# A three-stage transformer kernel on one core: the prologue and the first token tile rebuilt, with the second product of that tile in float32

## The chip, the cores and the metric

The kernel runs on one NeuronCore of a Trainium2 chip. The metric is the device time of one execution in microseconds. Five engines work side by side, each through its own instructions in order: TensorE (PE in the profile; PEld is its weight load), VectorE (DVE), ScalarE (ACT), GpSimd (POOL) and SyncE (SP), which here issues all the transfers between device memory and the chip. An instruction that has to wait holds up everything behind it on its engine.

## The reference

All inputs are float32. B = 8, S = 576 tokens, 8 heads of 64, model width 512, inner width 1024. Cut to what is computed:

```python
q_c = q.reshape(B, H, 9, 64, D)                  # k, v likewise: attention inside chunks of 64 tokens
scores = scale * q_c @ k_c.T; scores -= max(scores)
attn = exp(scores); attn /= sum(attn) + 1e-9
x = (attn @ v_c), heads side by side             # [B, S, 512]

h = max(x @ w_in, 0)                             # stage two, 512 -> 1024
conv_out = sum over k of conv_w[k] * h shifted by k - 1 tokens
x = (h * sigmoid(conv_out)) @ w_out              # 1024 -> 512

h = max(x @ w_in2, 0); u, v = halves of h        # stage three
x = (u * (w_spatial @ layernorm(v) + b_spatial)) @ w_out2
```

## The kernel before

**Products.** A float32 product is made of three products in the rounded type float32r: a matrix is kept as a rounded high part and a low part (the full value less the high part), and a product is high·high + low·high + high·low. The high part is a ScalarE copy (`nc.scalar.copy`, L127, L428, L353), the low part a subtraction (`split_lo`, L68) on VectorE or GpSimd.

**Weights.** They arrive as 64-bit words and are converted on the chip, in pieces of 128 x 512 (`Pieces`, L102): a load into `raw` (L111), a ScalarE scaling into `nr` (L78), two VectorE steps, a shift (L82) and a shift-and-or (L86), together called a merge here, and then the high and the low part. `w1` is the matrix of x @ w_in, `w2` that of the product behind the gate; eight pieces each. `w3` and `w4` belong to stage three.

**Phase A** does attention and stage two, `phase_b` stage three. Phase A walks through 11 token tiles of 384 or 448 tokens; a tile takes 8 slots, one for each 128 columns of the inner width. In slot s, `moe_in` does 12 matmuls into `h` (L381), `moe_h` (L387) makes on ScalarE max(h, 0) (L393) and the middle tap (L395), and on VectorE the outer two taps (L408); one slot later `moe_g` does tanh on ScalarE (L419) and the gate's product on VectorE (L420); a slot later `moe_split` makes the parts `gh`, `gl`; and in slot s + 3 (`LAG`) `moe_out` adds 12 matmuls into four accumulators `acc` (L441).

**Attention** goes by groups of 128 tokens, three or four groups a tile, and runs ahead of the tiles: `att_s` (scores on TensorE, L197), `sm1_steps` (row maximum, L210, then for the first six groups only a scaled negative maximum, L214, and for later ones a subtraction, L217), `att_exp` (for the first six groups eight ScalarE instructions with that bias, L233; one instruction for later ones, L237), `sm2_steps` (sum L247, a small constant L250, reciprocal L253, scaling L256), a transposition (`att_tp` on TensorE, L292, with a ScalarE copy, L296, for the first six groups; VectorE and eight transfers, L265 and L274, for later ones) and `att_pv` (L333 or L346), whose result `xh`, `xl` feeds `moe_in`.

**Order.** The order on every engine is the order of the code. A prologue (from L471) issues the loads, dummy matmuls on zeros (`keep_warm`, L467), the attention of groups 0 to 2 and the first pieces of w1. `start_slot` (L552) writes slots 0 to 8, in which the weights of stage two are still being converted: in slot s piece s + 1 of w1 and piece s - 1 of w2, roughly. In these slots the low parts of w1, w2 and g are subtractions on GpSimd, and the third tap of the convolution is a ScalarE product (L403) and a GpSimd addition (L413). The tables `S_SLOT` and `PV_SLOT` (L46) say in which slot the scores and the last product of groups 3 to 8 stand. Later slots are written by the loop at L579.

Of the kernel before, what the change touches and what calls it, by code (L numbers as in the profile page):

```python
# [7 lines left out]
F32 = mybir.dt.float32  # L8
# [10 lines left out]
DM = 512  # L19
# [21 lines left out]
LAG = 3  # L41
AHEAD = 3
VBUFS = 4
NP = 6
RBUFS = 5
S_SLOT = {3: 0, 4: 1, 5: 2, 6: 6, 7: 8, 8: 10}  # L46
# [14 lines left out]
def attention_moe_kernel(ctx: ExitStack, tc: tile.TileContext, qT, kT, vL, vP, eye, w1, cw, w2, w3, wsp, wsr, bsp, w4, out):  # L61
# [40 lines left out]
    class Pieces:  # L102
        def __init__(self, pool, items, bufs=2, nbufs=2):
            self.pool, self.items, self.bufs, self.nbufs = pool, items, bufs, nbufs
            self.raw, self.scaled, self.merged = [], [], []

        def load(self, n=1):
            for _ in range(min(n, len(self.items))):
                src, a, m, h, l = self.items.pop(0)
                raw = self.pool.tile([128, a, m], U64, tag="raw", name="raw", bufs=self.bufs)  # L110
                nc.sync.dma_start(out=raw, in_=src)  # L111
                self.raw.append((raw, a, m, h, l))

        def scale(self, n=1):
            for _ in range(min(n, len(self.raw))):
                raw, a, m, h, l = self.raw.pop(0)
                self.scaled.append((scale_word(self.pool, raw, a, m, self.nbufs), h, l))

        def merge(self, n=1):
            ps, self.scaled = self.scaled[:n], self.scaled[n:]  # L120
            self.merged += [(w[0], h, l) for w, h, l in ps]
            return merge_steps(*[w for w, _, _ in ps])

        def split(self, eng=nc.gpsimd):
            while self.merged:
# [18 lines left out]
    def phase_a(mid):  # L144
# [6 lines left out]
        es_st = ExitStack()  # L151
        st = es_st.enter_context(tc.tile_pool(name="start", bufs=1, side="right"))
# [7 lines left out]
        w2l = wp.tile([128, KF, DM], F32R, name="w2l")  # L160

# [25 lines left out]
        def att_s(g):  # L187
# [4 lines left out]
            else:  # L192
                ps = d["ps"] = ps_a.tile([128, 512], F32, tag="x" if g == 4 else "s", name="s").rearrange("p (u k) -> p u k", k=64)
# [8 lines left out]
        def sm1_steps(g):  # L202
# [18 lines left out]
            return [top, bias if g < NP else sub]  # L221
# [4 lines left out]
        def att_exp(g):  # L226
# [12 lines left out]
        def sm2_steps(g):  # L239
# [3 lines left out]
            sm = ap.tile([128, 8, 1], F32, tag="sm", name="sm")  # L243
# [32 lines left out]
            return [total, eps, inverse, norm]  # L276
# [4 lines left out]
        def att_tp(g):  # L281

            if g < NP:
# [5 lines left out]
                else:  # L289
                    tp = ps_h.tile([128, 512], F32, tag="h", name="tp")  # L290
# [621 lines left out]
```

## Time and profile before

| what | before |
|---|---|
| time, median of 3 runs (lowest to highest) | 954.9 us (953.62 to 955.35) |
| time of the profiled execution | 955.75 us |
| its span, first to last instruction | 954.0 us |
| busy: TensorE, VectorE, ScalarE, GpSimd | 927.8, 600.3, 441.0, 77.2 us |
| mean granted clock of TensorE, share of full | 0.989 |
| first 200 us: TensorE busy | 177.9 us |
| chain that ended last: TensorE, VectorE, transfers | 89%, 6%, 2% |

The busy times overlap, as the engines work side by side. What sets the end is read from the chain of waits, which is followed back from the last instruction, and from the stretches of the span in which TensorE, which is busy for 97% of it, is not.

### The profile page before, as it was taken

What the parts mean: (1) busy time and instruction counts of PE and PEld (TensorE: products, weight loads), DVE (VectorE), ACT (ScalarE), POOL (GpSimd) and SP (SyncE); (2) the same over time, 40 slices, a digit from 0 to 9 for tenths busy, and PEclk for the clock granted to TensorE, in tenths of its full rate; (3) what the DMA queues carried; (4) which work ended last, traced back from release to release, by engine and by line L of the source; (5) the groups of instructions that cost most, each with busy time, mean ns of one, the idle gap of its engine ahead of it and who ended that gap; (6) DMA issues with size and microseconds to landing.
All of it is one profiled execution on the core that took longest, in us unless ns stands there. A gap on an engine that the chain in (4) does not pass through costs nothing.

```text
span 954.0 us, 17696 instructions
## 1 busy us (share of the span) xinstructions
PE 927.8 (97%) x7002; PEld 852.3 (89%) x7002; DVE 600.3 (63%) x1221; ACT 441.0 (46%) x904; POOL 77.2 (8%) x100
## 2 busy tenths in 40 slices
PE   6788999999999999999999999999999999999998
PEld 6677899999999999999999898989898898989896
DVE  5997788989878777878656476361707263542522
ACT  5875356646554545454556454342323333332321
POOL 1673001101000000000000020010001000000000
PEclk8999899999999999999999999999999999999999
DMA  9833366445453434331303440203020302020001
GB/s 299 268 111 89 88 164 163 109 104 130 91 131 81 117 83 112 82 92 28 81 20 93 158 117 26 69 18 102 9 82 14 115 13 82 13 64 15 23 23 56
DMA packets 156754, 84.28 MB, mean 88 GB/s; under 512 B 81152, under 2 KB 144256, under 8 KB 156544
## 3 DMA queue, kind: packets, MB, share of 16 engines
q1 hardware_dynamic: 156672, 83.16, 32.1%
q8 instruction: 55, 0.90, 0.4%
q14 instruction: 27, 0.22, 0.1%
HBM read 54.29 MB, written 18.87 MB: 77 GB/s over the span
## 4 chain that ended last, share of the span: by engine, by line
PE 89%; DVE 6%; DMA 2%; SPq 1%; ACT 1%; issue 1%; ACTq 0%
PE h L381 20%; PE acc L441 19%; PE pss L786 12%; PE psu L752 11%; PE pso L805 11%; PE psv L700 10%; PE x L346 3%; PE s L197 3%; DMA raw<-in_w_dram 2%; DVE c L408 1%; DVE nr L86 1%; DVE raw L82 1%; DVE c L420 1%; SPq L274 1%; DVE e L256 0%
## 5 line engine op out<-in xcount | busy, mean ns | idle before, releaser
L408 DVE SCALAR_TENSOR_TENSOR c<-hh,nr,c 128x192 f32<-128x192 f32 (+20 forms) x272 | 124.8, 506 | 73.9 <-ACT c L395 72.8
L788 DVE TENSOR_TENSOR gf<-pss,bb 128x288 f32<-128x288 f32 x64 | 29.0, 453 | 146.0 <-PE pss L786 146.0
L393 ACT ACTIVATE hh<-h 128x450 f32<-128x450 f32 (+2 forms) x88 | 46.1, 524 | 107.3 <-PE h L381 106.9
L381 PE MATMUL h<-xh,w1h 128*128 128x450 f32 (+2 forms) x352 | 88.4, 374 | 2.4 <-ACT xh L353 1.3
L381 PE MATMUL h<-xh,w1l 128*128 128x450 f32 (+2 forms) x352 | 84.1, 361 | 1.5 <-POOL w1l L68 1.5
L381 PE MATMUL h<-xl,w1h 128*128 128x450 f32 (+2 forms) x352 | 84.5, 363 | 0.8 <-DVE xl L68 0.8
L441 PE MATMUL acc<-gl,w2h 128*128 128x384 f32 (+2 forms) x352 | 81.5, 353 | 1.1 <-POOL gl L68 1.1
L441 PE MATMUL acc<-gh,w2h 128*128 128x384 f32 (+2 forms) x352 | 81.9, 354 | 0.0
L441 PE MATMUL acc<-gh,w2l 128*128 128x384 f32 (+2 forms) x352 | 81.5, 353 | 0.0
L419 ACT ACTIVATE c<-c 128x384 f32<-128x384 f32 (+2 forms) x88 | 49.3, 560 | 57.0 <-DVE c L408 50.6
L786 PE MATMUL pss<-wsh,vl 128*128 128x288 f32 x256 | 75.4, 295 | 0.0
L786 PE MATMUL pss<-wsh,vh 128*128 128x288 f32 x256 | 75.4, 294 | 0.0
L786 PE MATMUL pss<-wsl,vh 128*128 128x288 f32 x256 | 75.3, 294 | 0.0
L381 PEld LDWEIGHTS h<-xh,w1l 128*128 128x128 f32 x352 | 66.7, 194 | 6.1 <-POOL w1l L68 2.8
L790 ACT CAST gth<-gf 128x288 fp32r<-128x288 f32 x64 | 27.7, 433 | 95.5 <-DVE gf L789 95.5
L381 PEld LDWEIGHTS h<-xl,w1h 128*128 128x128 f32 x352 | 67.1, 195 | 4.3 <-DVE xl L68 1.1
L381 PEld LDWEIGHTS h<-xh,w1h 128*128 128x128 f32 x352 | 63.1, 193 | 8.1 <-ACT xh L353 1.6
L441 PEld LDWEIGHTS acc<-gl,w2h 128*128 128x128 f32 x352 | 64.5, 188 | 5.0 <-POOL gl L68 2.1
L441 PEld LDWEIGHTS acc<-gh,w2h 128*128 128x128 f32 x352 | 65.1, 190 | 3.1
L441 PEld LDWEIGHTS acc<-gh,w2l 128*128 128x128 f32 x352 | 64.6, 188 | 3.0
L68 DVE TENSOR_TENSOR gl<-c,gh 128x448 fp32r<-128x448 f32 (+2 forms) x80 | 48.4, 605 | 17.1 <-ACT gh L428 17.1
L395 ACT ACTIVATE c<-hh,nr 128x384 f32<-128x384 f32 (+2 forms) x88 | 56.9, 646 | 3.0
(118 smaller groups left out, 1833.5 us busy)
## 6 DMA issues: line engine op xcount, KB each, us to landing
raw<-in_w_dram SPq DMA_DIRECT2D x28, 512.0 KB, 5.1
q<-in_qT_dram SPq DMA_DIRECT2D x33, 256.0 KB, 4.2
k<-in_kT_dram SPq DMA_DIRECT2D x33, 256.0 KB, 4.4
out_dram<-o SPq DMA_DIRECT2D x32, 256.0 KB, 2.1
v<-in_vL_dram SPq DMA_DIRECT2D x27, 256.0 KB, 3.9
pt<-t SPq DMA_DIRECT2D x216, 32.0 KB, 2.0
x2f<-x2d SPq DMA_DIRECT2D x24, 288.0 KB, 3.3
raw<-x2d SPq DMA_DIRECT2D x8, 288.0 KB, 2.9
```

The lines of the kernel that those rows point to most:

```text
L68: eng.tensor_tensor(out=lo, in0=full, in1=hi, op=ALU.subtract)
L381: nc.tensor.matmul(ph, wt[:, k, f * 128:(f + 1) * 128], x[:, k, :w], start=n == 0, stop=n == 11)
L393: nc.scalar.activation(out=h, in_=ph, func=AF.Relu)
L395: nc.scalar.activation(out=c, in_=h[:, o:o + n], func=AF.Copy, scale=cws[:, 1, f:f + 1])
L408: nc.vector.scalar_tensor_tensor(out=c[:, a:z], in0=h[:, o + a + step:o + z + step], scalar=cws[:, tap, f:f + 1], in1=c[:, a:z], op0=ALU.m ...
L419: nc.scalar.activation(out=c, in_=c, func=AF.Tanh, scale=0.5)
L441: nc.tensor.matmul(accs[m], w[:, f, m * 128:(m + 1) * 128], x, start=f == 0 and j == 0, stop=f == KF - 1 and j == 2,)
L700: nc.tensor.matmul(ps, x[:, k, sl], w[:, k, DV:], start=i == 0, stop=i == 11)
L752: nc.tensor.matmul(ps[:, :HB], w[:, k, d * 128:(d + 1) * 128], x[:, k, t], start=i == 0, stop=i == 11)
L786: nc.tensor.matmul(o, a[:, ds], w, start=i == 0, stop=i == len(mm) - 1)
L788: nc.vector.tensor_tensor(out=gf, in0=o, in1=bb[:, t], op=ALU.add)
L805: nc.tensor.matmul(ps, x[:, k, sl], w[:, k, :], start=i == 0, stop=i == 11)
```

## The change

It rewrites the prologue, slots 0 to 8 and what hangs on them:

- The second product of tile 0 is one float32 product: `moe_out` takes the gate's result `c` and a float32 matrix `w2f` (4 matmuls a slot for 12), with a lag of two slots (`LAG0`). `moe_split` falls away for tile 0. ScalarE scales the w2 pieces straight into `w2f`; their parts `w2h`, `w2l` are made later, one piece in each of slots 9 to 16, the low part on GpSimd.
- In slots 0 to 8 GpSimd does nothing else any more: the low parts of w1 are VectorE subtractions, and both outer taps of the convolution are VectorE instructions.
- Softmax: only group 1 keeps eight exponentials with a bias; these also give the row sums. The other early groups take a subtraction on VectorE and one exponential.
- Loads: q and k of groups 0 to 2 stand ahead of the first w1 piece. Dummy matmuls: 18, 6, 12, 3 and 4 for 22, 4 and 8.
- Scores of groups 3 to 8 stand in slots 1, 3, 5, 7, 8, 9 for 0, 1, 2, 6, 8, 10, and each slot's VectorE work comes in a new order.
- The conversion of w3 begins at slot 18 for 9; it and the reloading of stage two's result have pools of their own.

The diff, cut to its core:

```diff
+LAG0 = 2
+ACC = (1,)
-S_SLOT = {3: 0, 4: 1, 5: 2, 6: 6, 7: 8, 8: 10}
+S_SLOT = {3: 1, 4: 3, 5: 5, 6: 7, 7: 8, 8: 9}
...
+        def part(self, f, h, l, eng=nc.gpsimd):
+            nc.scalar.copy(out=h, in_=f)
+            split_lo(eng, l, f, h)
+
+        def high(self):
+            f, h, l = self.merged.pop(0)
+            nc.scalar.copy(out=h, in_=f)
+            self.lows.append((l, f, h))
+
+        def low(self):
+            while self.lows:
+                split_lo(nc.vector, *self.lows.pop(0))
...
-            return [top, bias if g < NP else sub]
+            return [top, bias if g in ACC else sub]
...
-            if g < NP:
+            if g in ACC:
...
                     nc.scalar.activation(
-                        out=e[:, i, :], in_=ps[:, i, :], func=AF.Exp, scale=SCALE, bias=mx[:, i, :]
+                        out=e[:, i, :], in_=ps[:, i, :], func=AF.Exp, scale=SCALE, bias=mx[:, i, :],
+                        accum_out=sm[:, i, :],
                     )
...
-            for wt, x in terms if s > KF else (terms[0], terms[2], terms[1]):
+            for wt, x in terms if s > KF or s == 0 else (terms[0], terms[2], terms[1]):
...
-            late = []
-            if s < KF:
...
+            between()
             for tap, step, segs in ((0, -1, prev), (2, 1, nxt)):
...
-            for a, z in late:
-                nc.gpsimd.tensor_tensor(out=c[:, a:z], in0=c[:, a:z], in1=c2[:, a:z], op=ALU.add)
...
-            split_lo(nc.gpsimd if s < KF else nc.vector, gl, g, gh)
+            split_lo(nc.vector, gl, g, gh)
...
+            if i == 0:
+                terms = [(w2f, gs.pop(s))]
+            else:
+                gh, gl = gs.pop(s)
+                terms = [(w2h, gh), (w2l, gh), (w2h, gl)]
...
-        def scores(s, now=True):
...
         def start_slot(s):
             ready = pv_at.get(s, [])
             moe_in(s)
+            products(s)
...
+            if s >= 1:
+                n = len(first.scaled)
+                if n:
+                    weave(first.merge())
+                moe_g(s - 1)
+                if first.merged:
+                    first.high()
+                if n > 1:
+                    weave(first.merge())
+            for g in due(s, "exp"):
+                att_exp(g)
+            for g in due(s, "sm2"):
+                att_sm2(g)
+            for g in at.get(s, []):
+                att_sm1(g)
             for g in ready:
                 att_tp(g)
...
+            if s >= LAG0:
+                moe_out(s - LAG0)
+            moe_h(s, first.low)
             for g in ready:
                 att_pv(g)()
                 load_v(g + VBUFS)
-            products(s)
-            moe_h(s)
-            scores(s, s + 1 == START)
+            first.load(2)
+            first.scale(2 if s < KF - 2 else 1)
...
+            if first.wait:
+                first.part(*first.wait.pop(0))
+            elif s > 2 * KF and s % 3 == 0:
                 later.turn()
```

How the order moves is shown at three places. The first is VectorE in slot 3 of tile 0, one of the eight slots in which pieces are converted; before, it reads (`raw`, `nr`: a weight piece; `mx`, `sm`, `rs`, `e`: softmax; `c`, `hh`: gate and convolution; `xl`: low part of the attention's result):

```order
L210 TENSOR_REDUCE mx<-s 128x8
L247 TENSOR_REDUCE sm<-e 128x8
L214 TENSOR_SCALAR mx<-mx 128x8
L250 TENSOR_SCALAR sm<-sm 128x8
L82 TENSOR_SCALAR raw<-raw 128x512
L253 RECIPROCAL rs<-sm 128x8
L82 TENSOR_SCALAR raw<-raw 128x512
L256 TENSOR_TENSOR e<-e,rs 128x512
L86 SCALAR_TENSOR_TENSOR nr<-nr,raw 128x512 x2
L420 SCALAR_TENSOR_TENSOR c<-c,hh 128x384
L68 TENSOR_TENSOR xl<-px,xh 128x4x64 x2
L408 SCALAR_TENSOR_TENSOR c<-hh,nr,c 128x383
```

and with the change:

```order
L86 TENSOR_SCALAR raw<-raw 128x512
L90 SCALAR_TENSOR_TENSOR nr<-nr,raw 128x512
L436 SCALAR_TENSOR_TENSOR c<-c,hh 128x384
L86 TENSOR_SCALAR raw<-raw 128x512
L90 SCALAR_TENSOR_TENSOR w2f<-w2f,raw 128x512
L232 TENSOR_REDUCE mx<-s 128x8
L239 TENSOR_TENSOR e<-s,mx 128x512
L71 TENSOR_TENSOR w1l<-nr,w1h 128x4x128
L426 SCALAR_TENSOR_TENSOR c<-hh,nr,c 128x383 x2
L71 TENSOR_TENSOR xl<-px,xh 128x4x64 x2
```

The two halves of a softmax now stand in alternating slots, the gate's product stands behind the first merge, and a w1 subtraction and a second tap are new here.

The second place is ScalarE in slot 3. Before (`w1h`, `w2h`, `gh`: high parts; `pt`: transposed scores):

```order
L393 ACTIVATE hh<-h 128x384
L395 ACTIVATE c<-hh,nr 128x384
L403 ACTIVATE c_606<-hh,nr 128x383
L296 COPY pt<-tp 128x512
L127 CAST w1h<-nr 128x4x128
L127 CAST w2h<-nr 128x512
L428 CAST gh<-c 128x384
L233 ACTIVATE e<-s,mx 128x64 x8
L419 ACTIVATE c<-c 128x384
L78 ACTIVATE nr<-raw 128x512 x2
L353 CAST xh<-px 128x4x64 x2
```

and with the change:

```order
L435 ACTIVATE c<-c 128x384
L137 CAST w1h<-nr 128x4x128
L321 COPY pt<-tp 128x512
L418 ACTIVATE hh<-h 128x384
L420 ACTIVATE c<-hh,nr 128x384
L378 CAST xh<-px 128x4x64 x2
L82 ACTIVATE nr<-raw 128x512
L82 ACTIVATE w2f<-raw 128x512
```

Four kinds of instruction are gone, and the scalings of the next two pieces now stand behind the copies of `px`.

The third place is TensorE around slot 3 (with the change; `acc` are the accumulators of the second product):

```order
L406 MATMUL h<-xl,w1h 128x384 x4
L406 MATMUL h<-xh,w1l 128x384 x4
L219 MATMUL s<-k,q 64x64 x16
L317 MATMUL tp<-idt,e 128x128 x4
L462 MATMUL acc_508<-c,w2f 128x384
L462 MATMUL acc_509<-c,w2f 128x384
L462 MATMUL acc_510<-c,w2f 128x384
L462 MATMUL acc_511<-c,w2f 128x384
L358 MATMUL px<-pt,v 64x64 x16
```

where before it read:

```order
L381 MATMUL h<-xh,w1h 128x384 x4
L381 MATMUL h<-xl,w1h 128x384 x4
L381 MATMUL h<-xh,w1l 128x384 x4
L292 MATMUL tp<-idt,e 128x128 x4
L441 MATMUL acc_670<-gh,w2h 128x384
L441 MATMUL acc_671<-gh,w2h 128x384
L441 MATMUL acc_672<-gh,w2h 128x384
L441 MATMUL acc_673<-gh,w2h 128x384
L441 MATMUL acc_670<-gh,w2l 128x384
L441 MATMUL acc_671<-gh,w2l 128x384
L441 MATMUL acc_672<-gh,w2l 128x384
L441 MATMUL acc_673<-gh,w2l 128x384
```

The scores stand in this slot now, four float32 matmuls stand where twelve stood (the last four, `gl` by `w2h`, follow behind the piece shown), and the product `px` waits behind them.

## Rows read from the trace of the kernel before

**Rows 1.** Windows: us, then busy time (instructions) per engine, granted clock, DMA share, GB/s.

```profile
60.00:70.00 10.00, 8.04 (x69) 6.81 (x69) 10.00 (x10) 7.04 (x15) 8.22 (x7) 1.00 0.27 78
70.00:80.00 10.00, 7.26 (x55) 6.11 (x55) 8.76 (x13) 5.84 (x14) 8.02 (x7) 0.83 0.10 28
...
104.00:124.00 20.00, 19.32 (x213) 18.55 (x212) 17.15 (x39) 10.84 (x22) 0.00 (x0) 1.00 0.52 137
...
204.00:300.00 96.00, 96.00 (x878) 90.72 (x877) 80.95 (x177) 51.69 (x101) 5.36 (x9) 1.00 0.47 109
```

**Rows 2.** Timeline, TensorE: start, length, instructions, in brackets idle before and releaser.

```profile
22.19 1.65 PE L381 MATMUL h<-xh,w1h 128*128 128x384 f32 x4 [0.47 <-ACT xh L353]
...
69.02 0.60 PE L292 MATMUL tp<-idt,e 128*128 128x128 f32 x4
...
72.26 0.68 PE L333 MATMUL px<-pt,v 64*64 64x64 f32 x16
...
97.69 1.97 PE L197 MATMUL s<-k,q 64*64 64x64 f32 x32 [3.47 <-DVE e L217]
```

**Rows 3.** Timeline, VectorE, first and last first-tile convolution, and instructions between them.

```profile
27.20 0.62 DVE L408 SCALAR_TENSOR_TENSOR c<-hh,nr,c 128x383 f32<-128x383 f32 x1 [1.59 <-ACT c L395]
...
35.74 1.21 DVE L250 TENSOR_SCALAR sm<-sm 128x8 f32<-128x8 f32 x1
...
59.59 3.48 DVE L86 SCALAR_TENSOR_TENSOR nr<-nr,raw 128x512 uint32<-128x512 uint32 x2
...
76.87 0.70 DVE L408 SCALAR_TENSOR_TENSOR c<-hh,nr,c 128x383 f32<-128x383 f32 x1
```

**Rows 4.** Groups by line and form, first 110 us, GpSimd: busy us, mean ns, idle before.

```profile
L68 POOL TENSOR_TENSOR w2l<-nr,w2h 128x512 fp32r<-128x512 f32 x8 | 12.3, 1547 | 0.0
...
L68 POOL TENSOR_TENSOR w1l<-nr,w1h 128x512 fp32r<-128x512 f32 x8 | 11.2, 1396 | 21.0 <-ACT w1h L127 21.0
...
L68 POOL TENSOR_TENSOR gl<-c,gh 128x384 fp32r<-128x384 f32 x8 | 10.4, 1298 | 2.4 <-ACT gh L428 2.4
...
L413 POOL TENSOR_TENSOR c<-c,c 128x383 f32<-128x383 f32 x8 | 8.1, 1014 | 17.1 <-DVE c L408 14.2 <-ACT gh L428 2.8
```

**Rows 5.** Chain of waits in order of time (start, length, what), one exponential of the prologue.

```profile
14.62 1.66 ACT e L233 x8
```

**Rows 6.** Timeline, TensorE, first scores.

```profile
6.65 1.15 PE L197 MATMUL s<-k,q 64*64 64x64 f32 x32 [1.04 <-DMA k<-in_kT_dram]
```

**Rows 7.** Timeline, VectorE, while GpSimd is idle.

```profile
17.02 0.17 DVE L250 TENSOR_SCALAR sm<-sm 128x8 f32<-128x8 f32 x1
...
18.08 0.42 DVE L82 TENSOR_SCALAR raw<-raw 128x512 uint32<-128x512 uint32 x1
18.53 0.69 DVE L86 SCALAR_TENSOR_TENSOR nr<-nr,raw 128x512 uint32<-128x512 uint32 x1
19.14 0.75 DVE L68 TENSOR_TENSOR xl<-px,xh 128x256 fp32r<-128x256 f32 x2
...
83.45 0.68 DVE L210 TENSOR_REDUCE mx<-s 128x8 f32<-128x512 f32 x1
...
84.78 0.55 DVE L420 SCALAR_TENSOR_TENSOR c<-c,hh 128x384 f32<-128x384 f32 x1
...
93.64 0.68 DVE L247 TENSOR_REDUCE sm<-e 128x8 f32<-128x512 f32 x1
...
95.53 0.71 DVE L265 STREAM_TRANSPOSE t<-e 128x512 f32<-128x512 f32 x1
```

**Rows 8.** Chain of waits in order of time, TensorE back to back.

```profile
82.12 1.08 PE s L197 x32
83.20 2.33 PE h L381 x12
85.53 2.12 PE acc L441 x12
...
99.66 4.16 PE h L381 x12
```

More of the change, by code (lines that the diff above doesn't have):

```diff
@@ L411, in moe_h @@
                     )
-            for a, z in late:
-                nc.gpsimd.tensor_tensor(out=c[:, a:z], in0=c[:, a:z], in1=c2[:, a:z], op=ALU.add)
             gs[s] = (h[:, o:o + n], c)
@@ L442, in moe_out @@
                         accs[m], w[:, f, m * 128:(m + 1) * 128], x,
-                        start=f == 0 and j == 0, stop=f == KF - 1 and j == 2,
+                        start=f == 0 and j == 0, stop=f == KF - 1 and j == len(terms) - 1,
                     )
@@ L457, in phase_a @@
         p1 = w_in_pieces(w1, w1h, w1l, range(KF))
-        p2 = w_out_pieces(w2, w2h, w2l)
-        first = Pieces(st, p1[:2] + [p for pair in zip(p1[2:], p2) for p in pair] + p2[KF - 2:], RBUFS, 5)
+        p2 = [(*p, w2f[:, k:k + 1, :]) for k, p in enumerate(w_out_pieces(w2, w2h, w2l))]
+        first = Pieces(st, p1[:2] + [p for pair in zip(p1[2:], p2) for p in pair] + p2[KF - 2:], RBUFS, 3)
         warm = st.tile([128, 256], F32, name="warm")
@@ L469, in keep_warm @@
                 )
+        load_qk(0)
+        load_qk(1)
+        load_qk(2)
         first.load()
-        for g in range(3):
-            load_qk(g)
         idt = wp.tile([128, 128], F32, name="idt")
@@ L478, in phase_a @@
         load_v(0)
+        first.load()
         load_v(1)
-        first.load()
         load_v(2)
@@ L486, in phase_a @@
         load_qk(4)
-        keep_warm(22)
-        first.scale()
-        weave(first.merge())
+        keep_warm(18)
         att_s(0)
-        first.split()
         att_sm1(0)
@@ L506, in phase_a @@
         att_sm2(1)
-        keep_warm(8)
+        weave(first.merge())
+        first.high()
         att_tp(1)
         x0 = att_pv(0)
-        weave(merge_steps(cw_words))
+        x1 = att_pv(1)
+        keep_warm(3)
         att_sm2(2)
         att_tp(2)
-        weave(first.merge())
-        first.load(2)
-        first.scale(2)
-        x0()
-        x1 = att_pv(1)
-        x2_ = att_pv(2)
-        x1()
-        x2_()
+        keep_warm(4)
+        x0()
+        x1()
+        first.low()
+        x2_ = att_pv(2)
+        first.scale()
+        x2_()
+        weave(merge_steps(cw_words))
+        first.load(2)
         load_qk(5)
@@ L541, in products, with due @@
                 load_qk(g + 3)
-        def scores(s, now=True):
-            for g in at.get(s, []):
-                if now:
-                    att_sm1(g)
-                else:
-                    todo.setdefault((s + 1, "sm1"), []).append(g)
                 todo.setdefault((s + 1, "exp"), []).append(g)
-                todo.setdefault((s + 2, "sm2"), []).append(g)
+                todo.setdefault((s + 1 if s < START else s + 2, "sm2"), []).append(g)
+        def due(s, what):
+            return todo.pop((s, what), [])
         def start_slot(s):
@@ L612, in phase_a @@
                 es_at.close()
+                es_lp.close()
                 mid()
-                x2s = [f for b in range(2) for f in x2_parts(b, mp, "raw", 2)]
+                x2p = es.enter_context(tc.tile_pool(name="x2p", bufs=1))
+                x2s = [f for b in range(2) for f in x2_parts(b, x2p)]
                 x2l = [f() for f in x2s[:2]]
```

98 lines of the change are left out of this document (46 added, 52 removed).

## The prediction

> **What bounds the kernel now.** I read the windows first. From 204 to 300 us TensorE is busy throughout, and for 19.32 of 20 us from 104 on, at full clock; VectorE has slack at 204 [rows 1]. Earlier this is not so: from 60 and from 70 us TensorE is busy for 8.04 and 7.26 of 10 us, and in the second the granted clock drops to 0.83 [rows 1]. A change to the prologue and the first tile can therefore pay only by letting TensorE's unbroken work begin earlier. I take as its beginning the input product of slot 11; the scores ahead of it wait 3.47 us for VectorE [rows 2].
>
> The timelines say what holds up the start. From the first convolution at 27.20 us to that of slot 7 at 76.87 us, 49.7 us for seven slots, VectorE is hardly ever idle (two entries between these two rows, 1.5 us together), but its instructions are stretched: a sum of 128 x 8 numbers takes 1.21 us and two shift-and-or steps take 3.48 us [rows 3], where the same take 0.17 and 0.69 us each while GpSimd is idle [rows 7]. GpSimd is busy for 8.2 of 10 us in the window from 60 us [rows 1], with 32 instructions of 1.0 to 1.5 us, 42.0 us together [rows 4]. The reader sees in one pair of rows that GpSimd's work is paid for on VectorE.
>
> **Prologue.** Dummy matmuls and scores: the first scores wait 1.04 us for q and k behind a weight piece [rows 6]; with q and k first, up to 1.04 us goes. A group's eight exponentials take 1.66 us in the chain [rows 5]; one instruction over the same 512 columns takes about as long as one VectorE pass, 0.7 us [rows 7], against which the subtraction costs some 0.5 us more than the small scaling did: net 0.5 us. The first w1 piece now arrives later and its merge, 0.42 + 0.69 us started 18.08 to 19.14, so 1.06 us [rows 7], stands ahead of group 2's sums: minus 1.06 us. ScalarE no longer makes the third tap, a pass of the tap's size (0.62 us on VectorE [rows 3]). The 12 matmuls of slot 0 began at the lower of the two clock levels, four in 1.65 us [rows 2]; of a later slot, twelve took 4.16 us at that level and 2.33 us at full clock [rows 8]. With 43 dummy matmuls for 34 I give the full clock about even odds; it is worth 1.8 us, but VectorE's work for the second piece hides part. Between 1.1 us (no clock gain) and 4.5 us I take 3.0: the first convolution starts at 24.2 us. The sums that come with group 1's exponentials show in no row; between nothing and 8 more instructions of 0.2 us, the ScalarE queue there has room until the merge. The later loads of the fifth and following pieces wait for a merge that is now 2 us later; they are wanted some 10 us after they land, so I cost them nothing.
>
> **Slots 0 to 7, VectorE.** Before, its work between the two convolutions, at the undisturbed prices [rows 7], and 0.62 for a tap [rows 3]: 12 merges of 1.06, 7 taps of 0.62, 7 gate products of 0.55, the first halves of four softmaxes (three at 0.85, one at 1.33, from 83.45 to 84.78), three second halves at 1.89 (93.64 to 95.53), three xl pairs at 0.75: 32.8 us. Add 1.5 us idle, and 15.4 us of the 49.7 are blocking by GpSimd. With the change: 13 merges 13.8, 14 taps 8.7, 7 gate products 3.9, four first halves at 1.33 5.3, three second halves 5.7, two xl pairs 1.5, and six w1 subtractions. These show in no VectorE row; between the 0.55 of a 384-column instruction and the 0.75 of two at 256 I take 0.65, since they have 512 columns: 3.9. The sum is 42.8 us. So 10.0 us of work are added and 16.9 us of blocking and idling go: the stretch shrinks by 6.9 us.
>
> **The same stretch, TensorE.** Seven input products at 2.33 us [rows 8] make 16.3, four sets of scores at 1.08 [rows 8] 4.3, three times tp and px at 0.60 + 0.68 [rows 2] 3.8. The float32 product of 128 x 128 by 384 columns shows in no row. The nearest are the scores, float32 of 64 x 64 by 64: 32 instructions, two for a product, in 1.08 us, 34 ns for 64 columns. If they ran one after another, 384 columns would take two times 0.20 us and four products 1.6 us; if two of these quarter-size products ran side by side, the full-size one takes twice that, 3.2 us. These are the ends, and I take 2.9, near the upper one, since a full-size product leaves no free part of the array, and a little below it for the start of each short instruction. Twelve float32r matmuls took 2.12 us [rows 8], so this product is no saving on TensorE. Six of them lie in the stretch: 17.4. The sum, 41.8 us, is level with VectorE's 42.8. The Trainium skill ("FP8 and Floating Point Precision", TensorE Precision Notes) speaks against the product as well: true float32 takes four passes. An estimate from it and the 12 matmuls above is 16 passes for 12, 2.8 us, and the sum would be 41.2; no row here shows the product itself.
>
> ScalarE loses the third tap, two casts a slot and seven exponentials of each early group; it was busy for 5.8 to 7.0 of 10 us in slots of 7.1 us [rows 1], so it sets nothing by itself, but it stands in the coupling below. Transfers: 0.27 and 0.10 of the engines in those windows [rows 1], no bound.
>
> **From slot 7 to slot 11.** The convolution of slot 7 starts at 24.2 + 42.8 = 67.0 us (76.87 before). VectorE then needs two taps, an xl pair, a merge, a gate product, a second half with the transposition (0.71) and a first half: 1.24 + 0.75 + 1.06 + 0.55 + 1.89 + 0.71 + 1.33 = 7.5 us, until 74.5; the next scores wait for that buffer. Behind them TensorE has scores 1.08, slot 9's input product 2.33, a float32 product 2.9, slot 10's input 2.12, px 1.08 (taken as the scores) and scores 1.08, 10.6 us. Slot 11's input product starts at 85.1 us. Before, its scores started at 97.69 and took 1.97 [rows 2], so it started at 99.6, and ran for 4.16 us at the lower clock instead of about 2.2 [rows 8]. The gain there is 14.5 + 2.0 = 16.5 us.
>
> **Slots 9 to 16.** Eight w2 low parts are now made here on GpSimd, 1.55 us each [rows 4]. In the first tile 15.4 us were blocked by some 38 us of GpSimd work that lay in the stretch, 0.4 us for each; eight times 1.55 gives 5.0 us on VectorE. It had about 15% of slack against TensorE later on, 80.95 of 96 us [rows 1], some 6 us in these eight slots, and w3's merges no longer fall here. I cost 1.5 us, with ends at nothing and 6. Eight ScalarE casts more are hidden in its slack, and the later start of w3, the new pools and the reloading are costed at nothing, as TensorE is closed there [rows 1]; were the reloading late, the end of phase A would show it.
>
> **Sum.** 16.5 - 1.5 = 15.0 us. Against the profiled execution's 955.75 us that is 940.75; the median of the runs is 0.85 us lower, so 940.0 us.
>
> **The rivals.** (1) *Float32 at the lower end.* At 1.6 us a slot TensorE needs 34.0 us in the stretch and the px copies never wait; only VectorE's 42.8 remains, and its overlap (each duration above holds some 0.08 us that the next one shares) shows: 4 us more, 936. For: no row rules it out. Against: the scores are small enough to share the array.
>
> (2) *VectorE takes TensorE's place after slot 9.* The w2 splits each block VectorE for their whole 1.55 us, 12.4 us, against 6 us of slack: 5 us of the gain go, 946 us. For: the 1.21 us of the 128 x 8 sum [rows 3]. Against: over the first tile only 0.4 us were blocked for each GpSimd microsecond. The Trainium skill ("SBUF — State Buffer", Who interferes with whom) has this as a rule: the port pair that the two engines share is locked for the whole instruction, and the other fully blocks. The trace agrees for single instructions (1.21 against 0.17 us).
>
> (3) *TensorE is closed, but at the lower clock.* In the ring of an odd slot px waits behind the float32 product, the copies of px wait for it, the scalings stand behind them on ScalarE, and the next merge and w1 cast wait for these. With TensorE busy for 7.26 of 10 us the clock was lower before, 0.83 [rows 1]. At half clock the stretch's 41.8 us are 83.6. If a fifth of the work runs so, TensorE needs 50.2 us, 7.4 more than VectorE: 947.4 us. If half does, it needs 62.7 us, 19.9 more: 960, slower than before. The point from which it decides is where the loss eats the 15 us, 38% of the stretch's work at the lower level. Against: TensorE's work is 98% of VectorE's there, and from 60 us, with TensorE busy for 8.04 of 10, the clock was full [rows 1].
>
> **How the numbers follow.** The forecast, 937 to 944, has 0.60; rival 1 0.12, rival 2 0.11, rival 3 in its mild form 0.10, in its slow form 0.04, and 0.03 lies between these two, near no change. The range from 935 to 948.5 takes in the forecast, rivals 1 and 2 and half of the mild third, some 0.87 at its face and less with what I have not thought of. A measurement of this kernel can tell about 0.2%, 1.9 us: faster 0.93, the same 0.03, slower 0.04.
>
> **What would show it.** Right: no GpSimd row from 10 to 66 us; shift-and-or at 0.6 to 0.7 us throughout; convolutions of slots 0 and 7 near 24 and 67 us; float32 matmuls that make 2.7 to 3.0 us a slot; the slot-11 product near 85 us at full clock. Wrong: VectorE waits of over 0.5 us a slot for ScalarE's scalings (rival 3's ring), a granted clock below 0.9 between 30 and 70 us, or new TensorE waits for VectorE between 85 and 130 us (rival 2).

## The result and the profile after

| what | before | after |
|---|---|---|
| time, median (lowest to highest), 4 runs each | 954.33 us (953.62 to 955.35) | 940.06 us (939.18 to 940.40) |
| profiled execution; its span | 955.75; 954.0 us | 940.28; 938.5 us |
| busy: TensorE, VectorE, ScalarE, GpSimd | 927.8, 600.3, 441.0, 77.2 us | 923.6, 598.4, 427.4, 47.8 us |
| mean granted clock | 0.989 | 0.998 |

The ratio is 0.9848, with an interval of 0.9831 to 0.9865: 14.3 us, 1.5%, faster. The forecast was 940.0. Between the two profiled executions, 15.5 us apart, TensorE's busy time fell by only 4.2 us and VectorE's by 1.9; the other 11.3 us are idle time of TensorE that went.

The windows of after, with the columns of [rows 1]:

```profile
30.00:40.00 10.00, 7.90 (x62) 6.08 (x63) 9.58 (x20) 5.06 (x11) 0.00 (x0) 1.00 0.89 284
60.00:70.00 10.00, 9.18 (x96) 6.84 (x95) 8.63 (x18) 5.05 (x11) 0.00 (x0) 1.00 0.20 56
70.00:80.00 10.00, 10.00 (x97) 7.73 (x97) 6.63 (x15) 3.30 (x7) 0.00 (x0) 1.00 0.41 99
104.00:124.00 20.00, 19.21 (x211) 18.36 (x211) 19.28 (x35) 11.44 (x23) 5.17 (x5) 1.00 0.37 81
```

In 60 to 70 and 70 to 80 us TensorE was busy for 8.04 and 7.26 us, the second at a clock of 0.83 [rows 1]; now it is 9.18 and 10.00, at full clock. VectorE has the place of the bottleneck at 30 us: 9.58 of 10 us, GpSimd nothing. From 104 to 124 us the other side shows: VectorE went from 17.15 to 19.28 of 20 us, and TensorE's share is no better than before.

The timeline of after, VectorE, with the first-tile convolutions of slots 0 and 7 and, between them, a w1 subtraction with the instruction behind it:

```profile
24.88 1.27 DVE L426 SCALAR_TENSOR_TENSOR c<-hh,nr,c 128x383 f32<-128x383 f32 x2 [0.35 <-ACT c L420]
...
42.08 0.68 DVE L71 TENSOR_TENSOR w1l<-nr,w1h 128x512 fp32r<-128x512 f32 x1
42.68 1.26 DVE L426 SCALAR_TENSOR_TENSOR c<-hh,nr,c 128x383 f32<-128x383 f32 x2
...
66.69 1.27 DVE L426 SCALAR_TENSOR_TENSOR c<-hh,nr,c 128x383 f32<-128x383 f32 x2 [0.27 <-ACT c L420]
```

The stretch between them is 41.8 us, where it was 49.7 [rows 3]. Nothing in it is stretched any more: every shift-and-or of the 13 takes 0.69 us, where two took 3.48 [rows 3]. Between the first and the last of these rows VectorE waited for another engine once, 0.27 us just ahead of the last. The chain of waits runs through VectorE alone from 24.88 to 62.3 us, and from there to 78.7 through TensorE, with one ScalarE copy of 0.68 us. From 79.9 to 119.0 us it runs mostly through VectorE again, and for some 10 us through the queue of the transfers; its last step back to TensorE reads:

```profile
118.16 0.70 DVE e L239
...
119.00 1.15 PE s L219 x32
```

The timeline of after, TensorE, the answer to [rows 2, 8]:

```profile
7.88 3.57 PE L219 MATMUL s<-k,q 64*64 64x64 f32 x64 [1.47 <-DMA k<-in_kT_dram]
...
21.27 0.96 PE L406 MATMUL h<-xh,w1h 128*128 128x384 f32 x4 [0.47 <-ACT xh L378]
...
45.30 2.75 PE L462 MATMUL acc<-c,w2f 128*128 128x384 f32 x8
47.58 1.16 PE L406 MATMUL h<-xh,w1h 128*128 128x384 f32 x4
...
64.83 2.75 PE L462 MATMUL acc<-c,w2f 128*128 128x384 f32 x8
67.51 0.98 PE L358 MATMUL px<-pt,v 64*64 64x64 f32 x32
...
72.41 2.85 PE L462 MATMUL acc<-c,w2f 128*128 128x384 f32 x8
75.19 1.15 PE L219 MATMUL s<-k,q 64*64 64x64 f32 x32
...
83.31 1.15 PE L371 MATMUL x<-pt,v 64*64 64x64 f32 x32
85.24 1.15 PE L219 MATMUL s<-k,q 64*64 64x64 f32 x32 [0.78 <-DVE e L239]
86.32 0.99 PE L406 MATMUL h<-xh,w1h 128*128 128x386 f32 x4
...
88.56 0.87 PE L462 MATMUL acc<-gh,w2h 128*128 128x384 f32 x4
```

Slot 0's four matmuls take 0.96 us for 1.65. Slot 11's input product begins at 86.32 us (99.59 before) and runs at full clock. The float32 product is 8 instructions for 4 products; the next product begins 2.28 us after it where that is an input product, 2.68 where it is `px` and 2.78 where it is scores.

### The profile page after: what moved, and what is told of

Read it like the earlier page. It is cut to its first block, busy times and chain, and to the rows that moved or that the text cites. A ratio compares the mean times of both kernels' runs of the same rounds, so it can differ in the third digit from the quotient of the medians.

```text
span 938.5 us, 17588 instructions
## 1 busy us (share of the span) xinstructions
PE 923.6 (98%) x6979; PEld 842.0 (90%) x6979; DVE 598.4 (64%) x1236; ACT 427.4 (46%) x861; POOL 47.8 (5%) x76
## 4 chain that ended last, share of the span: by engine, by line
PE 89%; DVE 7%; DMA 1%; SPq 1%; ACT 1%; issue 1%; DVEq 0%; ACTq 0%
PE h L406 19%; PE acc L462 19%; PE pss L821 13%; PE psu L787 11%; PE pso L840 11%; PE psv L735 10%; PE x L371 3%; PE s L219 3%; DVE c L426 2%; DMA k<-in_kT_dram 1%; DVE nr L90 1%; DVE e L281 1%; DVE mx L232 1%; DVE raw L86 1%; SPq L299 0%
## 5 line engine op out<-in xcount | busy, mean ns | idle before, releaser
L426 DVE SCALAR_TENSOR_TENSOR c<-hh,nr,c 128x383 f32<-128x383 f32 (+20 forms) x280 | 137.0, 534 | 59.7 <-ACT c L420 58.2
L406 PE MATMUL h<-xl,w1h 128*128 128x450 f32 (+2 forms) x352 | 81.8, 354 | 0.0
L435 ACT ACTIVATE c<-c 128x384 f32<-128x384 f32 (+2 forms) x88 | 49.1, 558 | 68.2 <-DVE c L426 68.1
L462 PE MATMUL acc<-gh,w2h 128*128 128x448 f32 (+2 forms) x320 | 74.4, 354 | 0.0
L462 PE MATMUL acc<-gl,w2h 128*128 128x448 f32 (+2 forms) x320 | 74.4, 354 | 0.0
L462 PE MATMUL acc<-gh,w2l 128*128 128x448 f32 (+2 forms) x320 | 74.3, 354 | 0.0
L406 PEld LDWEIGHTS h<-xl,w1h 128*128 128x128 f32 x352 | 64.9, 188 | 3.2
L462 PEld LDWEIGHTS acc<-gh,w2h 128*128 128x128 f32 x320 | 59.1, 188 | 3.1
L462 PEld LDWEIGHTS acc<-gl,w2h 128*128 128x128 f32 x320 | 59.0, 188 | 2.8
L462 PEld LDWEIGHTS acc<-gh,w2l 128*128 128x128 f32 x320 | 58.9, 188 | 2.8
```

Source lines behind the costliest of these rows:

```text
L406: nc.tensor.matmul(ph, wt[:, k, f * 128:(f + 1) * 128], x[:, k, :w], start=n == 0, stop=n == 11)
L426: nc.vector.scalar_tensor_tensor(out=c[:, a:z], in0=h[:, o + a + step:o + z + step], scalar=cws[:, tap, f:f + 1], in1=c[:, a:z], op0=ALU.m ...
L435: nc.scalar.activation(out=c, in_=c, func=AF.Tanh, scale=0.5)
L462: nc.tensor.matmul(accs[m], w[:, f, m * 128:(m + 1) * 128], x, start=f == 0 and j == 0, stop=f == KF - 1 and j == len(terms) - 1,)
```

## The experiments

Times stand against before, which had 954.99 to 955.39 us beside these runs. After was timed only beside a before of 954.33 us, so a difference of about 1 us from after is not clear of noise: the intervals of the ratios of e1, e2, e4, e6 and e8 overlap that of after (0.9831 to 0.9865), and there the traces have to decide. The theory: in slots 0 to 7 VectorE sets the pace, by its own work and by what GpSimd blocks; the float32 product pays because work of VectorE and GpSimd goes with it, although TensorE saves nothing by it. That last part no run tests by itself, as e3 will show.

**GpSimd's work moved, nothing dropped (e3).** Before, with GpSimd's work and the third tap on VectorE:

```diff
-            if s < KF:
+            if False:
                 c2 = mp.tile([128, 64 * TILES[0]], F32, tag="c2", name="c2", bufs=2)
...
-            split_lo(nc.gpsimd if s < KF else nc.vector, gl, g, gh)
+            split_lo(nc.vector, gl, g, gh)
-        first.split()
+        first.split(nc.vector)
-            first.split()
+            first.split(nc.vector)
```

> The kernel before with one part of the change alone: everything that GpSimd did in slots 0 to 8 (low parts of w1, w2 and g, the addition of the third tap) is on VectorE, the float32 product is not there. Theory: VectorE's own work sets the stretch from the first convolution to that of slot 7; it grows from 32.8 us by 6 w1 and 7 w2 low parts at 0.61, some 6 low parts of g at 0.5 and 7 taps at 0.6, 15 us, to about 48, while the 15.4 us of blocking go: the stretch stays at 47 to 49.7 us and the time at 951 to 955. Rival (ending the blocking is the gain, the rest is detail): stretch 40 us or less, time 942 to 945.

Measured: 953.64 us, ratio 0.9987 [0.9976, 0.9999], first convolutions at 27.00 and 76.14 us. Its VectorE timeline shows what came for the stretching that went, a wait and three subtractions:

```profile
34.72 1.27 DVE L408 SCALAR_TENSOR_TENSOR c<-hh,nr,c 128x383 f32<-128x383 f32 x2 [1.60 <-ACT c L395]
...
59.78 0.69 DVE L68 TENSOR_TENSOR w1l<-nr,w1h 128x512 fp32r<-128x512 f32 x1
60.38 0.68 DVE L68 TENSOR_TENSOR w2l<-nr,w2h 128x512 fp32r<-128x512 f32 x1
...
62.86 0.55 DVE L68 TENSOR_TENSOR gl<-c,gh 128x384 fp32r<-128x384 f32 x1
```

The stretch is 49.1 us for 49.7: moving GpSimd's work, with the order left as it was, pays next to nothing. The theory's time came out, but not quite for its reason. VectorE waited 4.8 us for ScalarE between the two convolutions (1.5 in before, 0.3 in after), so its own work filled some 44 us and not 48. `w2l` and `gl` are 7.6 us of that (eight at 0.60 and six at 0.47 us to the next instruction), and the float32 product takes them away. But a better order might have taken away the waits as well: that alone would bring this stretch to 44.3 us at best, 4.8 of the 7.3 us that lie between this run and after. An estimate of what the product brings by itself is therefore 2.5 us, if order could do all of that, up to 7.6 us, since these instructions would come on top of a VectorE that is full in after. No run tells where between them it lies; it would take after with the split product of before.

**A cheaper second product (e2, e11).** After, with tile 0's second product as four float32r matmuls on `w1h` in place of `w2f` (this leaves the product with w2 out for tile 0):

```diff
-            nc.vector.scalar_tensor_tensor(out=c, in0=c, scalar=1.0, in1=h, op0=ALU.add, op1=ALU.mult)
-            gs[s] = c
+            g = c
+            if s < KF:
+                g = mp.tile([128, WMAX], F32R, tag="gh", name="gh", bufs=LAG)[:, :outputs(0)[1]]
+            nc.vector.scalar_tensor_tensor(out=g, in0=c, scalar=1.0, in1=h, op0=ALU.add, op1=ALU.mult)
+            gs[s] = g
...
-                terms = [(w2f, gs.pop(s))]
+                terms = [(None, gs.pop(s))]
...
-                        accs[m], w[:, f, m * 128:(m + 1) * 128], x,
+                        accs[m], w1h[:, m, 0:128] if w is None else w[:, f, m * 128:(m + 1) * 128], x,
```

> The changed kernel with the second product of tile 0 as four float32r matmuls a slot (the high part of w1 stands in for the weights, so this leaves the second product of tile 0 out; its place and its waits for the gate stay): 0.7 us for 2.3 to 2.7 a slot on TensorE. Theory (VectorE sets slots 0 to 7, TensorE only from slot 8): the convolution of slot 7 moves by at most 1 us, and 2 to 4 us come from slots 8 to 10: 936 to 938. Rival (TensorE is level and sets the odd slots): 8 x 2 = 16 us less work, at least 8 us faster, 932 or below.

Measured: 941.75 us, 0.9868 [0.9852, 0.9884], not faster than after, against both expectations. The stretch stayed at 41.8 us (24.20 to 65.96): a product of 0.7 us in place of 2.3 to 2.7 changes nothing there, so VectorE alone sets it. Then the slots behind it lost what they could have gained; TensorE in this run:

```profile
83.46 1.97 PE L219 MATMUL s<-k,q 64*64 64x64 f32 x32 [2.67 <-DVE e L239]
85.36 1.65 PE L406 MATMUL h<-xh,w1h 128*128 128x386 f32 x4
...
89.38 0.87 PE L465 MATMUL acc<-gh,w2h 128*128 128x384 f32 x4
```

and its windows:

```profile
40.00:50.00 10.00, 6.84 (x64) 5.75 (x62) 9.65 (x20) 6.17 (x13) 0.00 (x0) 1.00 0.88 276
50.00:60.00 10.00, 8.83 (x93) 8.24 (x94) 9.62 (x20) 7.07 (x15) 0.00 (x0) 0.83 0.47 138
80.00:90.00 10.00, 7.33 (x76) 7.10 (x71) 8.04 (x16) 5.40 (x12) 3.78 (x4) 0.66 0.47 121
```

The scores start 1.78 us earlier than in after (83.46 for 85.24), but wait 2.67 us for VectorE, and what follows runs at the lower level: 1.90 us to the next product for 1.08, and 4.02 for 2.24 (85.36 to 89.38). Slot 11's product so ends 0.8 us later than in after.

The same edit with the order of e10, the last experiment below (e11):

> The changed kernel with two edits: the softmax halves of the later slots in the order of e10, and tile 0's second product as four float32r matmuls on w1's high part in place of w2f, as in e2 (it leaves that product out). It asks why e2 was no faster. Theory (up to the convolution of slot 7 VectorE alone sets the pace, and only the two products that stand behind it, some 1.7 us cheaper each, can pay): first-tile stretch 41.5 to 42.5 us, 933.5 to 936.5 us. Rival (the float32 product keeps TensorE's clock up, and without it the lower clock takes the gain and more): granted clock below 0.9 between 80 and 100 us, 937 to 941 us. Second rival (TensorE sets the pace of the first tile): stretch below 40 us, under 932 us.

Measured: 936.49 us, 0.9806 [0.9792, 0.9819], the same as with that order alone (936.44). The stretch is 41.8 us again (23.78 to 65.55). The gain of the two late products again goes into waits. VectorE's subtraction and TensorE's next scores and product:

```profile
72.21 0.69 DVE L239 TENSOR_TENSOR e<-s,mx 128x512 f32<-128x512 f32 x1
```

```profile
73.00 1.15 PE L219 MATMUL s<-k,q 64*64 64x64 f32 x32 [1.74 <-issue]
74.08 1.36 PE L406 MATMUL h<-xh,w1h 128*128 128x386 f32 x4
```

The scores come 1.74 us after TensorE was free; the profile names no releaser ("issue"), but they come right behind that subtraction, which ends at 72.90. Slot 9's product then takes 3.7 us at the lower level (clock 0.83 from 70 to 80 us, full from 80 on). At slots 11 and 12 this run is still 1.3 us ahead of e10, and loses that to a wait of 0.78 us for VectorE at the scores of 93.78 us. So the clock fell elsewhere than this rival had it, and VectorE is what holds the path.

**What a GpSimd subtraction costs VectorE (e1, e7, e12).** After, w1's low parts on GpSimd:

```diff
-                split_lo(nc.vector, *self.lows.pop(0))
+                split_lo(nc.gpsimd, *self.lows.pop(0))
...
-                first.split(nc.vector)
+                first.split(nc.gpsimd)
```

> The changed kernel with one part undone: the low parts of w1 go back to GpSimd, eight subtractions of 1.4 us. Theory (a GpSimd subtraction blocks VectorE for about 0.4 us per microsecond in the mean): 0.6 us comes off VectorE for each and 0.4 to 0.6 comes back as blocking, and w1l is ready later for TensorE: 939 to 942. Rival (the whole instruction blocks VectorE): 6 x 0.8 = 5 us slower, 945. Rival (GpSimd is free once it has little to do): 3.6 us faster, 936.5.

Measured: 942.14 us, 0.9870 [0.9855, 0.9885]; stretch 44.1 us (24.54 to 68.60). On VectorE the shift-and-or beside the split takes 1.70 us, the other one 0.69:

```profile
46.07 0.69 DVE L90 SCALAR_TENSOR_TENSOR nr<-nr,raw 128x512 uint32<-128x512 uint32 x1
...
47.61 1.70 DVE L90 SCALAR_TENSOR_TENSOR w2f<-w2f,raw 128x512 uint32<-128x512 uint32 x1
```

The split of 1.27 us started at 47.49, so it blocked 1.01 us, against 0.60 that the subtraction costs on VectorE itself: 0.4 us a slot. The stretch has six such splits (0.96 to 1.04 us each), which makes 2.5 us against 2.3 measured. The time lies 0.1 us above the theory's range, and nearly 3 us or more from both rivals.

After, the w2 low parts of slots 9 to 16 on VectorE (e7):

```diff
-                first.part(*first.wait.pop(0))
+                first.part(*first.wait.pop(0), nc.vector)
```

> The changed kernel with one edit: the eight w2 low parts of slots 9 to 16 are VectorE subtractions, so that GpSimd is idle from 10 to 200 us but for the four small copies of tile 1. Theory: a subtraction costs VectorE 0.6 to 0.7 us of its own, where a GpSimd one held up its taps by about 1 us (2.43 for 1.40); some 0.3 us a slot come free, part of TensorE's 2.0 us of waits for the softmax subtractions goes, 938.5 to 940.3 us. Rival (the prediction's second: GpSimd blocks VectorE for its whole 1.5 us): 0.9 us a slot come free, all of the 2.0 us go, 937 to 938.3 us. Second rival (VectorE is the bound there by its own work): slower, above 941 us.

Measured: 937.89 us, 0.9819 [0.9805, 0.9832]: the first rival's time, 2.2 us less than after. TensorE's waits for the scores after 70 us fall from 2.0 to 0.8 us. A wait costs more than its idle time: between the input products of slots 12 and 13, for one, after takes 6.90 us with a wait of 0.38 us, this run 6.31 without one. Three waits that went so make 1.8 of the 2.2 us. The taps of one slot, in after and then in this run:

```profile
90.10 2.43 DVE L426 SCALAR_TENSOR_TENSOR c<-hh,nr,c 128x193 f32<-128x193 f32 x4
```

```profile
88.06 0.68 DVE L71 TENSOR_TENSOR w2l<-w2f,w2h 128x512 fp32r<-128x512 f32 x1
...
90.20 1.39 DVE L426 SCALAR_TENSOR_TENSOR c<-hh,nr,c 128x193 f32<-128x193 f32 x4
```

A split of about 1.4 us blocks 1.04 us, not its whole length, for 0.60 on VectorE. The time fits the rival, its price per split doesn't.

The edits of e7 and e10 together (e12):

> The changed kernel with the edits of e10 and e7 together: the softmax halves reordered, the w2 low parts on VectorE. Theory: with e10's order TensorE waits for nothing from 70 us on, so cheaper work on VectorE has nothing left to give, 936.0 to 937.0 us (e10: 936.44). Rival (the GpSimd splits still cost time): 934 to 935.5 us.

Measured: 936.53 us, 0.9806 [0.9792, 0.9819], as with the order alone: once TensorE waits for nothing, a cheaper VectorE has nothing to give.

**Dummy matmuls (e9).** After, with only the first 18 of 43:

```diff
-        keep_warm(6)
...
-        keep_warm(12)
...
-        keep_warm(3)
...
-        keep_warm(4)
```

> The changed kernel with the 18 dummy matmuls at the start alone, the 25 between the attention steps left out. Theory (they hold the clock up for slot 0): the clock is at its lower level when slot 0's input product runs, 4.1 us for 2.3, the first convolution 1 to 2 us later, 941 to 942.5. Rival (VectorE's work for the second piece hides it): 940, with the lower clock in the windows from 10 to 30 us.

Measured: 943.33 us, 0.9879 [0.9865, 0.9894], 3.3 us more than after. The windows and slot 0 on TensorE:

```profile
10.00:20.00 10.00, 6.93 (x105) 5.73 (x101) 9.21 (x22) 6.83 (x27) 0.00 (x0) 0.67 1.07 352
20.00:30.00 10.00, 9.00 (x70) 8.56 (x72) 4.96 (x12) 5.17 (x10) 0.38 (x2) 0.59 0.81 241
```

```profile
22.62 1.65 PE L406 MATMUL h<-xh,w1h 128*128 128x384 f32 x4 [0.47 <-ACT xh L378]
```

The clock is 0.67 and 0.59 in the first two windows from 10 us, for 0.94 and 1.00 in after, and the first convolution starts at 28.04 for 24.88 us. The 25 dummies do work that nobody reads and bring some 3 us.

**Three orders of the prologue and the first tile.** The first w1 piece ahead of q and k (e4):

```diff
+        first.load()
         load_qk(0)
         load_qk(1)
         load_qk(2)
-        first.load()
```

> The changed kernel with the first w1 piece loaded ahead of q and k again, as before. Theory (the prologue goes by transfers; the first scores come 1.4 us later, and the piece is wanted only at 13 us): the first convolution 1 to 2 us later, 941 to 942. Rival (the rest of the prologue hides it): 940.

Measured: 941.21 us, 0.9857 [0.9842, 0.9872]; first convolution 25.32 us. The first scores start 1.4 us later (6.66 for 5.26), as the theory had it, and the time is 1.15 us longer; but the first convolution is only 0.4 us later than in after, and neither is clear of the scatter shown next. Group 1's softmax like the others (e8):

```diff
-ACC = (1,)
+ACC = ()
```

> The changed kernel with one edit: group 1's softmax like the other early groups (a subtraction on VectorE and one exponential, then a row sum on VectorE) in place of eight exponentials that give the row sums. Theory: VectorE, busy for 9.28 of 10 us from 10 to 20 us, stands on the chain there and gets a subtraction of 0.6 us and a sum of 0.6 to 0.7 us, less a small scaling of 0.2; ScalarE gets 1.7 us back, which nobody waits for; first convolution 25.3 to 26.0 us (after: 24.88), 940.5 to 941.3 us. Rival (the eight exponentials with their eight reads of the sums, 10.88 to 13.35 us, hold up the scalings of the next weight piece behind them): first convolution 23.8 to 24.6 us, 938.9 to 939.8 us.

Measured: 941.20 us, 0.9864 [0.9846, 0.9882]; first convolution 25.03 us. The time fits the theory, the convolution's 0.15 us doesn't, and the wait for k was 1.1 us longer in this run. Eight profiled executions share one prologue (after, e2, e5, e6, e7, e10, e11, e12), and their first convolutions lie between 23.76 and 25.06 us. What they differ in is when k arrives, and the clock: in five it is full from 8 to 12 us and the convolution starts at 23.76 to 24.20; in after, e7 and e12 some of the scores run at the lower level (in after the clock is 0.50 from 8 to 10 us) and it starts at 24.52 to 25.06. So this one stays undecided. The w1 low parts ahead of the softmax in a slot (e6):

```diff
+            first.low()
             for g in due(s, "exp"):
                 att_exp(g)
...
-            moe_h(s, first.low)
+            moe_h(s)
```

> The changed kernel with one move: in slots 1 to 8 the w1 low part stands on VectorE ahead of the softmax, not behind it. TensorE waited 2.9 us for it in slots 2, 3, 5 and 7. Theory (VectorE is full in these slots, so TensorE's waits there cost little): 0 to 1.5 us faster, 938.5 to 940. Rival (these waits are on the path): 2.9 us faster, 937.

Measured: 940.28 us, 0.9849 [0.9832, 0.9865], no change. The waits of the input product for `w1l` (2.9 us in after) are gone; a wait of `px` for VectorE of 1.6 us came, and in one window the lower clock:

```profile
40.00:50.00 10.00, 8.35 (x51) 6.91 (x48) 9.65 (x20) 6.13 (x13) 0.00 (x0) 0.83 0.89 274
```

The stretch is 0.9 us longer (42.7 us, 23.94 to 66.64), which does not show in the time because the first convolution starts 0.9 us earlier in this execution than in after's. On an engine that is always busy, order mainly chooses who waits.

**The slots behind the first tile.** Scores of group 8 in slot 10, as before the change (e5):

```diff
-S_SLOT = {3: 1, 4: 3, 5: 5, 6: 7, 7: 8, 8: 9}
+S_SLOT = {3: 1, 4: 3, 5: 5, 6: 7, 7: 8, 8: 10}
```

> The changed kernel with the scores of group 8 in slot 10, as before, for slot 9. Theory (before, these scores waited 3.47 us for VectorE and the clock fell behind the wait): the wait comes back in part, 2 to 4 us, and with it a lower clock: 942 to 946. Rival (VectorE is early enough now): 940.

Measured: 943.63 us, 0.9885 [0.9868, 0.9901], 3.6 us more: TensorE waits 4.0 us at once for a subtraction, and the clock is 0.92 and 0.91 from 80 to 100 us.

The last one swaps the halves of two softmaxes in the loop of the slots from 9 on (e10):

```diff
-            for g in due(s, "sm2"):
-                att_sm2(g)
             for g in at.get(s, []):
                 att_sm1(g)
+            for g in due(s, "sm2"):
+                att_sm2(g)
```

> The changed kernel with one move behind slot 8: the first half of a softmax (maximum and subtraction) stands on VectorE ahead of the second half of the softmax before it, so that the scores buffer is free 2.6 us earlier. TensorE waits 2.0 us in all, in four places, for that buffer, the only waits it has behind 70 us. Theory (these waits are on the path, since TensorE is closed behind them): 1.5 to 2 us faster, 938 to 938.6. Rival (the second half and its transfers are late instead, and the last product of attention waits): 939.5 to 941.

Measured: 936.44 us (935.97 to 937.44), 0.9809 [0.9795, 0.9824]: faster than before by 18.6 us and than after by 3.6, twice what was expected. TensorE waits for no other engine from 70 us on, and the chain of waits runs through it alone from there; a window, and the place that was shown for after at 83.31 to 86.32 us:

```profile
90.00:100.00 10.00, 10.00 (x111) 9.69 (x110) 9.64 (x20) 5.39 (x12) 2.87 (x2) 1.00 0.68 178
```

```profile
82.47 1.15 PE L371 MATMUL x<-pt,v 64*64 64x64 f32 x32
83.45 1.10 PE L219 MATMUL s<-k,q 64*64 64x64 f32 x32
84.48 0.98 PE L406 MATMUL h<-xh,w1h 128*128 128x386 f32 x4
```

The subtraction that the next scores wait for now stands ahead of the other group's sum and scaling, and the 2.0 us of waits are gone. They cost more than the 2.0 us: from `x` to the input product it is 2.01 us here and 3.01 in after, where the wait is 0.78; the three others cost 0.6 us for 0.4. That makes 2.8 us. The other 0.8 us between the two profiled executions are there at the first convolution already (24.03 for 24.88 us), within the scatter of the prologue. VectorE's timeline has one more change:

```profile
95.28 0.71 DVE L290 STREAM_TRANSPOSE t<-e 128x512 f32<-128x512 f32 x1
95.91 0.91 DVE L71 TENSOR_TENSOR gl<-c,gh 128x384 fp32r<-128x384 f32 x1
```

Three of the eight splits now lie beside a transposition and `gl`, where they cost 0.34 to 0.36 us (0.91 for 0.55) instead of 1.04. That helps VectorE to be early, but it is no gain besides the waits.

## Why the prediction was right

The mechanism was right: the start is held by VectorE, and TensorE's unbroken work begins 13.3 us earlier. That the sum came within 0.1 us is luck: its terms are off by up to 1.5 us and make up for each other.

- **First convolution: 24.2 us forecast, 24.88 found**, a gain of 2.3 for 3.0. The full clock came (0.96 us for the four matmuls) and is worth what was said or more, as the run without dummies shows. The term that was too large is the 1.04 us of the scores: they start 1.39 us earlier (5.26 us for 6.65 [rows 6]), but those of group 1 then wait 1.47 us for their k, and the 64 matmuls behind take 3.57 us, partly at the lower clock, so that the third group's end where they ended before (11.45 and 11.44 us). In the five executions with the full clock there, the first convolution is at 23.76 to 24.20 us. The row sums that showed in no row do now: eight extra instructions of 0.2 us.
- **Stretch: 42.8 us forecast, 41.8 found.** Its working holds in kind (no blocking, as GpSimd has two copies of 0.19 us and nothing else from 10 to 66 us; VectorE closed; 0.60 us of pace for a w1 subtraction taken at 0.65); the overlap of neighbours, 0.08 us each, which rival 1 named, makes most of the difference.
- **TensorE level with VectorE there: wrong.** It waited some 3.6 us in the stretch. The mis-sized term is the float32 product: 2.9 us taken, 2.28 to 2.68 found, 2.5 on average over the six, which is 2.5 of the 3.6 us. The Trainium skill ("FP8 and Floating Point Precision", TensorE Precision Notes) gives four passes, an estimate of 2.8 us; the measured 2.28 us is less.
- **Slot 7 to slot 11: 18.1 us forecast, 19.6 found.** The step "the next scores wait for that buffer" failed for the first scores: they started at 75.19 us right behind a float32 product, so TensorE set this piece (the chain says so from 62.3 to 78.7 us), 0.4 us behind VectorE's subtraction, which ends at 74.81. The second scores then did wait for VectorE, 0.78 us, which the sum had not. The full clock for slot 11 came: 2.24 us for 4.16 [rows 8], and the lead grows by 1.9 us from slot 11 to slot 12 (2.0 forecast).
- **Slots 9 to 16: a loss of 1.5 us forecast, 0.4 found.** The lead over before, taken at the starts of the same products, is 13.3 us at slot 11, 15.2 at slot 12, 14.8 at slot 17, and stays between 14.7 and 14.9 to the last products of stage three; the two spans differ by 15.5. VectorE did lose 1 us for each of seven splits, and TensorE waited 1.2 us for scores behind slot 11; but before waited there too, 0.9 us. The mechanism is there, its price against before was too high. Against what was possible it was too low: with all these waits gone (e10), TensorE gains 2.8 us.
- **The rivals.** Rival 1 is refuted: the product takes 2.28 us and more, and one far below 1.6 us (0.7 us a slot, e2 and e11) didn't make the kernel faster. Rival 2's mechanism is real, and its sign came: four new TensorE waits for VectorE between 85 and 119 us, 2.0 us together. VectorE takes the path there until 119.0 us. What the splits add to it is the 1.8 to 2.2 us of e7; blocking by the whole length is not what the rows show (1.04 of some 1.4 us). Rival 3's ring shows: ScalarE waited 1.43 us for `px` in slots 3 and 5, but VectorE had other work meanwhile; only in slot 7, where ScalarE waited 1.58 us, did VectorE's `xl` wait for it, 0.68 us. The clock stayed at 1.00 from 20 us on.

## What to carry to other kernels

Moving work off a side engine gave next to nothing here where it landed on the engine that sets the pace, with the order left as it was; look for work that can fall away there, even at the price of a dearer operation on an engine that waits, and count that engine's own waits before you credit either. Where two engines are nearly level, write first on the one what the other waits for next: swapping two softmax halves was worth 2.8 to 3.6 us here. Dummy matmuls in TensorE's gaps kept its clock up in the prologue, and a cheaper operation that opened gaps gave its gain back.

## What was not expected of the hardware

- **Less TensorE work, lower clock, no gain.** With the cheap product TensorE was busy for 6.84 of 10 us (9.75 in after) from 40 us, the clock fell to 0.83 in the next window and to 0.66 after a wait of 2.67 us. Such a row alone does not tell which way the clock goes: e11 has nearly the same busy time from 40 us, and its clock stayed full until 70 us. Why, the runs do not show.

```profile
40.00:50.00 10.00, 6.85 (x64) 5.83 (x64) 9.65 (x20) 6.00 (x13) 0.00 (x0) 1.00 0.87 274
50.00:60.00 10.00, 7.96 (x86) 6.72 (x82) 9.55 (x21) 7.26 (x15) 0.00 (x0) 1.00 0.44 134
```

- **What GpSimd blocks depends on VectorE's instruction beside it.** In after a split ran beside a transposition and a row maximum, and neither took longer than alone [rows 7]; the split itself took 1.72 us, while the taps beside another took 2.43 us for 1.40:

```profile
82.47 1.72 POOL L71 TENSOR_TENSOR w2l<-w2f,w2h 128x512 fp32r<-128x512 f32 x1 [60.49 <-ACT w2h L132]
86.34 1.49 POOL L71 TENSOR_TENSOR w2l<-w2f,w2h 128x512 fp32r<-128x512 f32 x1 [2.16 <-ACT w2h L132]
```

```profile
83.08 0.71 DVE L290 STREAM_TRANSPOSE t<-e 128x512 f32<-128x512 f32 x1
83.72 0.65 DVE L232 TENSOR_REDUCE mx<-s 128x8 f32<-128x512 f32 x1
...
85.95 2.43 DVE L426 SCALAR_TENSOR_TENSOR c<-hh,nr,c 128x193 f32<-128x193 f32 x4
```

  The Trainium skill ("SBUF — State Buffer", Who interferes with whom) says this in the part that the prediction left out: a VectorE instruction with at most one input in SBUF, outside the two-port modes, does not contend, and one with two does, whichever came first keeping the ports. These rows agree: `t` and `mx` read one operand, the taps read two. The constant added to 128 x 8 sums in [rows 3] reads one operand too and took 1.21 us for 0.17; by that rule it would have to run in a two-port mode, which no row here shows. It would also explain why some 0.4 us per GpSimd microsecond fitted the first tile and 0.7 (1.04 of 1.4 us) the later slots; which instructions lay beside each other there was not counted.
- **An accumulated sum is an instruction of its own.** ScalarE in after, one of group 1's eight exponentials:

```profile
11.19 0.30 ACT L257 ACTIVATE e<-s,mx 128x64 f32<-128x64 f32 x1
11.38 0.20 ACT L257 ACTIVATION_READ_ACCUMULATOR e<-s,mx 128x1 f32 x1
```
